# A fused attention and squared-ReLU kernel: its list of 4,011 steps is written anew

## The chip, the cores and the metric

One core of one Trainium2 chip runs the program. The metric is the device time of one execution in microseconds (us). Each engine takes its instructions strictly in the order in which the program lists them: TensorE (PE, matmuls), VectorE (DVE), ScalarE (ACT), GpSimd (POOL) and SyncE (SP, which issues every DMA). An instruction that waits for another engine holds up all that stands behind it on its own engine.

## The reference

Block-causal attention over 8 batches, 8 heads, 576 positions and 64 dimensions, then a two-layer network with a squared ReLU on its 4,608 rows:

```python
scores = scale * np.matmul(q, k.transpose(0, 1, 3, 2))
mask = block_i >= block_j                     # blocks of 64 positions
attn = softmax(np.where(mask, scores, -1e9))
x = np.matmul(attn, v)                        # rows of 8 heads x 64
h = x @ w_in                                  # 512 -> 2048
r = np.maximum(h, 0.0)
out = (r * r) @ w_out                         # 2048 -> 512
```

## The kernel before

Nearly all matmuls are in float16. A float32 operand is split into a high half and a low rest (`high`, then `low` = value - high), and three products replace one. Much of the work of DVE, ACT and POOL is this splitting.

**Attention** goes in passes of one batch and two heads; passes 0 to 11 (the first keys of batches 0 and 1, and their later keys for batch 0) stay in float32, the rest are split. Of pass `i` and part `n`: `A` are the scores on PE (into the PSUM tiles `side`), `B` the row maximum on DVE (`nmx`), `C` the exponential on ACT, `S` a small step on POOL (`sm`), `R` the reciprocal on DVE (`rs`), `H` and `L` the high and low halves of the probabilities (`p_rows`), `T` a DMA transpose, `G` the product with the values on PE (`px`), `X` its scaling into `x`. `fv`, `fa` to `fe`, `vh` and `vl` scale and split the values.

**Norm and split of a tile of x** (batch `b`, half `g`): `sq` and `sa` square and add (tile `sq`), `nq` sums on PE, `hb` makes a power of two, `xm` multiplies (`x<-x,hb`), then the halves `h` and `l` go to `xt_all`. From the fifth chunk on there are also the sums `s1` to `s4` (tile `s`), which either DVE or POOL makes.

**The first layer** works on twelve chunks of 384 rows. The first four are plain: `ph` (12 matmuls of 384 columns), `pos`, `sqr`, `top` (high half) and `rem` (low half, tile `hidden`). The other eight use seven products `p1` to `p7` in four groups in place of eight, each of 12 matmuls of 192 columns (tiles `group`): `c` copies a product out of PSUM into `r` (ACT or DVE), `a` adds the second product (DVE, `r<-group,rescale,r`), `sq` squares, `top` and `rem` split. `p6` waits for `c11`, `p5` for `a11`, `p7` for `c12`, `p4` for `c22`, `p3` for `a22`. The weights for this are made between chunks 1 and 3 by the steps `t`, on DVE or POOL (tile `_AluOpType.subtract`, then `turned_w` or `w`).

**The second layer** is `po` (three matmuls of 512 columns a step), `ob` (scaling) and `out` (store). The weights themselves are loaded and split at the start by `bits`, `prelu`, `join`, `max`, `cast` and `low`.

**What sets the order** is one string, `ORDER`: 4,011 names of steps, some with the engine behind a colon (`:D` DVE, `:A` ACT, `:P` POOL). `plan_all` registers each step with `add` (engine, length, predecessors `after`, rank, buffers), and `Plan.run` takes the steps out in the order of the string. It reads nothing of a step but the function that issues it:

```python
for word in ORDER.split():
    name, _, way = word.partition(":")
    make = self.tasks.pop(name)[3]
    make(WAYS[way]) if way else make()
```

`add` keeps predecessors and lengths in a record that `run` doesn't read. Every instruction is issued through one line of a helper, L329, so the profile tells steps apart by their tiles. On each engine the instructions are bound to the order of the string; waits between engines follow from the data.

Of the kernel before, what the change touches and what calls it, by code (L numbers as in the profile page):

```python
# [108 lines left out]
r11 Q4:A r12 r13 r14 r15 bits0_10 keys9 bits0_11 max0_10 bits0_13 B8_0 E6 G5 C8_0 hb0_0 S8_0 cast0_0:P E7 clear F6:A B8_1 C8_1 max0_11 S8_1 max0_12
X5_0:A load8 G6 Q5:A bits0_12 max0_13 F7:A max0_14 z0 xm0_0 A8_2 prelu0_7 X6_0:A max0_15 Q6:A G7 w0a1 h0_0 bits0_5 w0b1 X7_0:A Q7:A R8_0 nq1_0 B8_2  # L110
D8_0:A bits0_7 R8_1 w0c1 w0d1 C8_2 S8_2 keys10 l0_0 A9_0 D8_1:A w0e1 hb1_0 low0_0 E8_0_0 E8_0_2 A9_1 R8_2 F8_0_0:A D8_2:P cast0_1:P xm1_0 join0_5
F8_0_2:A E8_1_0 h1_0 B9_0 z1 E8_0_1 l1_0 F8_1_0:A F8_0_1:A bits0_9 E8_1_1 z2 prelu0_8 C9_0 F8_1_1:A B9_1 join0_7 ia1_0 E8_2_0 F8_2_0:A S9_0 w0e C9_1
S9_1 ph0_0 pos0_0 low0_1 bits0_14 E8_2_1 join0_8 A9_2 cast0_2:P R9_0 sqr0_0 F8_2_1:A A10_0 B9_2 join0_6 z3 z4 bits1_0 D9_0:A B10_0 C9_2 prelu0_9 S9_2
low0_2 R9_1 cast0_3:P join0_9 keys11 ph0_1 pos0_1 D9_1:D prelu0_10 R9_2 G8_1 D9_2:P join0_10 A10_1 low0_3 cast0_4:D prelu0_11 prelu0_12 ph0_2 E9_0_0
sqr0_1 top0_1:A C10_0 low0_4 X8_1:A S10_0 cast0_5:P join0_11 prelu0_13 bits1_3 B10_1 pos0_2 join0_12 join0_13 top0_0:D low0_5 E9_0_1 sqr0_2 F9_0_0:A
ph0_3 R10_0 C10_1 S10_1 cast0_6:P prelu0_14 E9_0_2 A10_2 A11_0 F9_0_2:D prelu0_15 join0_14 pos0_3 prelu1_0 bits1_1 F9_0_1:D D10_0:A bits0_15 bits1_2
load11 B10_2 ph0_4 C10_2 join1_0 low0_6 E9_1_0 F9_1_0:A E9_1_1 top0_2:D rem0_1 pos0_4 F9_1_1:A cast0_7:D join0_15 low0_7 sqr0_3 cast0_8:P load9 ph0_5
E9_2_0 E9_2_1 ph0_6 max1_0:A S10_2 R10_1 D10_1:D pos0_5 bits1_4 prelu1_1 F9_2_1:A B11_0 F9_2_0:A sqr0_4 A11_1 G9_1 low0_8 prelu1_2 R10_2 cast0_9:P
load12 join1_1 prelu1_3 E10_0_0 rem0_2 pos0_6 sqr0_6 z5 prelu1_4 D10_2:P ph0_7 C11_0 X9_1:A B11_1 max1_1:D F10_0_0:A E10_0_1 E10_0_2 bits1_5 join1_2
S11_0 prelu1_5 ph0_8 C11_1 pos0_7 low0_9 cast0_10:P F10_0_1:A F10_0_2:A rem0_0 E10_1_0 S11_1 max1_2:D join1_4 top0_6:D sqr0_7 R11_0 join1_3 D11_0:A  # L120
join1_5 low0_10 cast0_11:P max1_5:D R11_1 F10_1_0:A top0_7:D top0_4:D z6 bits1_6 E10_1_1 F10_1_1:A A11_2 sqr0_5 B11_2 A12_0 low0_11 cast0_12:P load10
top0_3:D E10_2_0 rem0_3 top0_5:A E10_2_1 C11_2 z7 bits1_7 F10_2_1:A prelu1_6 S11_2 ph0_9 z8 prelu1_7 pos0_8 pos0_9 F10_2_0:D G10_1 sqr0_8 E11_0_0
B12_0 prelu1_8 max1_4:A X10_1:A bits1_8 low0_12 F11_0_0:A cast0_13:P A12_1 D11_1:D E11_1_0 load13 R11_2 D11_2:P join1_6 z9 vals12 rem0_6 C12_0 E11_0_2
F11_1_0:A bits1_9 join1_7 prelu1_9 S12_0 F11_0_2:A max1_6:A rem0_4 ph0_10 z10 B12_1 E11_2_0 E11_2_1 max1_7:D F11_2_0:A ia0_0 C12_1 A12_2 low0_13
# [1900 lines left out]
```

## Time and profile before

| | us |
|---|---|
| median of three runs | 976.61 (975.47 to 978.28) |
| the profiled execution | 977.2 |
| its span | 975.4 |
| PE busy | 941.6 (97%) |
| DVE busy | 795.4 (82%) |
| ACT busy | 599.8 (61%) |
| POOL busy | 264.5 (27%) |

A view by stretches gives the busy time of each engine and the clock that was granted to PE as a share of the full one. A timeline row gives start, length, engine, operation, tiles, shape and count; in square brackets stands the idle time just before it and what ended it. A row of groups gives the busy time and the mean of one in ns.

### The profile page before, as it was taken

Reading aid. Unit: us, or ns where it says so; the run is one execution under the profiler, and the core shown is the slowest. Engines: PE = TensorE matmul, PEld = TensorE weight load, DVE = VectorE, ACT = ScalarE, POOL = GpSimd, SP = SyncE. Lnnn points to the kernel's source line nnn. Section 1 sums busy time; section 2 is a strip of 40 time slices with the busy share of each in tenths; the row PEclk is TensorE's granted clock in tenths of the full one; section 3 lists DMA queues with packets and bytes.
Section 4 is the critical chain, followed back from the end, with each engine's and each line's share of the span. In section 5 each row is a group of like instructions: output and inputs, shape, how many; then the busy total and the mean of one; then the engine's idle time right before and its main releaser. Section 6 shows DMA issues by size and latency. Waiting matters only on the chain.

```text
span 975.4 us, 20874 instructions
## 1 busy us (share of the span) xinstructions
PE 941.6 (97%) x8001; PEld 593.2 (61%) x8001; DVE 795.4 (82%) x1769; ACT 599.8 (61%) x1510; POOL 264.5 (27%) x366
## 2 busy tenths in 40 slices
...
GB/s 360 326 123 168 163 134 101 165 174 174 83 128 117 122 100 121 111 74 121 148 96 140 41 163 79 153 118 100 91 161 119 90 99 90 79 13 1 23 2 44
DMA packets 221649, 114.92 MB, mean 118 GB/s; under 512 B 195290, under 2 KB 203756, under 8 KB 221548
## 3 DMA queue, kind: packets, MB, share of 16 engines
...
## 4 chain that ended last, share of the span: by engine, by line
PE 72%; DVE 18%; DMA 4%; issue 3%; ACT 2%; POOL 1%; SPq 1%; DVEq 0%; POOLq 0%; ACTq 0%
PE pair L329 37%; PE group L329 21%; PE side L329 7%; DVE p_rows L329 5%; PE px L329 5%; DVE nmx L329 3%; DVE w L329 2%; PE po L329 2%; DMA first<-in_qk 2%; DVE r L329 2%; DVE hidden L329 1%; DMA hidden<-in_w_in 1%; ACT p L329 1%; DVE xt_all L329 1%; DVE x L329 1%
## 5 line engine op out<-in xcount | busy, mean ns | idle before, releaser
L329 PE MATMUL pair<-w,hidden 128*128 128x512 f16 (+1 forms) x1680 | 382.1, 377 | 1.6 <-DVE ob L329 1.6
L329 PEld LDWEIGHTS <-hidden 128*128 128x128 f16 x1776 | 169.5, 98 | 179.7 <-issue 11.8
L329 PEld LDWEIGHTS <-w 128*128 128x128 f16 x2304 | 201.4, 98 | 74.3 <-issue 16.3
L329 ACT ACTIVATE p<-side,nmx 128x256 f32<-128x256 f32 (+8 forms) x264 | 139.7, 538 | 111.7 <-DVE nmx L329 80.5
L329 POOL TENSOR_TENSOR hidden<-r,hidden 128x384 f16<-128x384 f32 x101 | 104.0, 1040 | 228.5 <-ACT hidden L329 216.0
L329 DVE SCALAR_TENSOR_TENSOR p_rows<-p,rs,p_rows 128x128 f16<-128x128 f32 (+6 forms) x264 | 147.5, 581 | 9.8 <-ACT p_rows L329 6.7
L329 PE MATMUL group<-xt_all,w 128*128 128x192 f16 x1536 | 142.9, 246 | 1.6 <-DVE r L329 1.4
L329 DVE TENSOR_REDUCE nmx<-side 128x1 f32<-128x192 f32 (+8 forms) x288 | 123.3, 479 | 18.5 <-PE side L329 18.0
L329 PE MATMUL pair<-xt_all,w 128*128 128x384 f16 x768 | 131.1, 326 | 2.0 <-ACT r L329 1.2
L329 POOL TENSOR_SCALAR sm<-sm 128x2 f32<-128x2 f32 (+2 forms) x104 | 34.3, 330 | 351.6 <-ACT p L329 337.2
L329 ACT ACTIVATE r<-r 128x384 f32<-128x384 f32 x208 | 106.8, 522 | 33.0 <-DVE r L329 30.5
L329 PE MATMUL group<-xt_all,turned_w 128*128 128x192 f16 x1152 | 108.9, 246 | 0.3 <-DVE r L329 0.3
L329 PEld LDWEIGHTS <-turned_w 128*128 128x128 f16 x1152 | 96.1, 98 | 12.2 <-issue 3.5
L329 PE MATMUL side<-qk 64*64 64x512 f32 (+2 forms) x480 | 97.2, 500 | 3.4 <-ACT p L329 1.9
L329 PE MATMUL side<-ks,qk 64*64 64x128 f32 (+4 forms) x576 | 92.3, 425 | 0.1
L329 ACT CAST hidden<-r 128x384 f16<-128x384 f32 x156 | 76.5, 508 | 19.3 <-DVE r L329 17.0
L329 DVE SCALAR_TENSOR_TENSOR r<-group,rescale,r 128x384 f32<-128x384 f32 x96 | 58.3, 612 | 33.7 <-PE group L329 26.8
L329 ACT ACTIVATE r<-group,rescale 128x384 f32<-128x384 f32 x72 | 41.4, 577 | 59.5 <-PE group L329 51.7
L329 ACT ACTIVATE p_rows<-p,rs 128x64 f16<-128x64 f32 (+9 forms) x124 | 61.9, 525 | 19.3 <-DVE rs L329 15.1
L329 DVE TENSOR_SCALAR p_rows<-p,rs 128x384 f16<-128x384 f32 (+9 forms) x156 | 68.6, 456 | 1.8 <-DMA p_turned<-p_rows 0.5
L329 PE MATMUL px<-p_turned,v 128*64 128x384 f16 (+5 forms) x1168 | 67.2, 269 | 1.7 <-ACT wt L329 1.4
L329 PEld LDWEIGHTS <-v 128*64 128x64 f16 x1128 | 49.1, 110 | 21.1 <-issue 8.8
...
## 6 DMA issues: line engine op xcount, KB each, us to landing
...
```

What stands on the lines that cost most here:

```text
L329: i = make(*a, **k)
```

## The change

The string is replaced by another with the same 4,011 names. Half of the names stand over 11 places from where they were, and some change engine: `c` 12 from DVE to ACT, `ob` 6 from DVE to ACT, `sq` 19 from ACT to DVE, `t` 12 and `s` 15 from DVE to POOL, `rem` 3 from DVE to POOL, `H` 16 from DVE to ACT. In all DVE has 1,355 steps where it had 1,410, ACT 944 for 919, and POOL 345 for 315. PE's steps are the same in number and kind. Five places of `plan_all` change what is passed to `add` as predecessors or freed buffers.

```diff
-p0 A0 B0 C0 S0 A1 r0 B1 C1 p1 prelu0_0 r1 A2 r2 prelu0_1 bits0_0 max0_0 S1 R0 prelu0_2 D0:D R1 D1:P p2 r3 B2 C2 bits0_1 A3 bits0_2 S2 bits0_3 B3 C3 E0
...
-                over = {x: [f"po{prev}_2_{4 * g + int(x[1]) + 1}"] for x in ("11", "12", "21", "22")}
+                over = {x: [f"po{prev}_{m}_{4 * g + int(x[1]) + e}" for m in ((0, 1), (1, 2))[int(x[0]) - 1] for e in (-1, 1)] for x in ("11", "12", "21", "22")}
...
-                    ends = [(opener, z) for z in ("xt0", "xt1")] if g == NQ - 1 else []
+                    ends = [(opener, z) for z in ("xt0", "xt1")]
...
-                over = [f"po{prev}_2_{f}"] if ck else []
+                over = [f"po{prev}_{m}_{f}" for m in range(3)] if ck else []
...
-            add(f"X{i}_1", {"ACT": 440, "DVE": 490}, 0, [f"G{i}_1"], base + YR[3], lambda q, t=t: values_out(t, 1, q), frees=[(f"G{i}_1", "x")])
+            add(f"X{i}_1", {"ACT": 440, "DVE": 490}, 0, [f"G{i}_1", "l1_0" if t["b"] == 0 else "l0_1"], base + YR[3], lambda q, t=t: values_out(t, 1, q), frees=[(f"G{i}_1", "x")])
...
-                        if hp == 0:
-                            pb = b - 1 if g else (b - 1 if b > NT else 0)
-                            past = ([f"l{pb}_{g}"] if plain(chunk_of(pb, g)) else [f"l23{pb}_{g}", f"l6{pb}_{g}"]) if pb >= 0 else []
-                        else:
-                            past = []
+                        pb = b - 1 if g else (b - 1 if b > NT else 0)
+                        past = ([f"l{pb}_{g}"] if plain(chunk_of(pb, g)) else [f"l23{pb}_{g}", f"l6{pb}_{g}"]) if pb >= 0 else []
```

The program built from the old code with the new string alone has the same instructions on every engine, row for row, as the one with all of the change.

**First place: POOL at some 397 to 408 us, between the second layer of chunk 4 and the first of chunk 3.** Tiles `t_AluOpType` and `w_107` are the weight steps `t`, `sm` the steps `S`, `s_3_0` the sums of a tile of x. Before:

```order
L329 TENSOR_SCALAR sm_0_0_4_4597<-sm_0_0_4_4597 128x4
L329 TENSOR_TENSOR t_AluOpType.subtract_4485<-t_AluOpType.subtract_4485,w_107 128x512
L329 TENSOR_SCALAR sm_0_0_7_4648<-sm_0_0_7_4648 128x3
L329 TENSOR_TENSOR w_107<-t_AluOpType.subtract_4483,w_107 128x2x256
L329 TENSOR_TENSOR w_107<-t_AluOpType.subtract_4485,w_107 128x2x256
L329 TENSOR_TENSOR s_3_0_4762<-x_97 128x192
L329 TENSOR_TENSOR s_3_0_4787<-s_3_0_4762,x_97 128x192
```

Now, on POOL at the same place of the program:

```order
L329 TENSOR_SCALAR sm_0_0_4_4595<-sm_0_0_4_4595 128x4
L329 TENSOR_TENSOR w_107<-t_AluOpType.subtract_4586,w_107 128x2x256
L329 TENSOR_SCALAR sm_0_0_7_4636<-sm_0_0_7_4636 128x3
L329 TENSOR_TENSOR w_107<-t_AluOpType.subtract_4463,w_107 128x2x256
L329 TENSOR_TENSOR s_3_0_4767<-x_97 128x192
L329 TENSOR_TENSOR s_3_0_4770<-s_3_0_4767,x_97 128x192
L329 TENSOR_TENSOR x_97<-x_97,s_3_0_4770 128x2x96
L329 TENSOR_TENSOR x_97<-x_97 128x2x96
```

Behind the step `S24_1` (`sm_0_0_7`) stand one weight step where there were two, and four sums of x where there were two.

**Second place: DVE at the same time, up to the sums `sq_0_0` that PE's step `nq3_0` waits for.** `p_rows` are the halves of the probabilities. Before:

```order
L329 RECIPROCAL rs_0_0_7_4664<-sm_0_0_7_4648 128x3
L329 TENSOR_SCALAR p_rows<-p_4_0_0_7_4647,rs_0_0_7_4664 128x512
L329 TENSOR_SCALAR p_rows<-p_4_0_0_7_4647,rs_0_0_7_4664 128x384
L329 SCALAR_TENSOR_TENSOR p_rows<-p_4_0_0_7_4647,rs_0_0_7_4664,p_rows 128x384
L329 SCALAR_TENSOR_TENSOR p_rows<-p_4_0_0_7_4647,rs_0_0_7_4664,p_rows 128x512
L329 SCALAR_TENSOR_TENSOR p_rows<-p_4_0_0_4_4596,rs_0_0_4_4627,p_rows 128x320
L329 TENSOR_TENSOR sq_0_0_4717<-sq_0_0_4717 128x384
L329 TENSOR_TENSOR sq_0_0_4717<-sq_0_0_4717 128x192
```

Now, on DVE at the same place of the program:

```order
L329 RECIPROCAL rs_0_0_7_4652<-sm_0_0_7_4636 128x3
L329 SCALAR_TENSOR_TENSOR p_rows<-p_4_0_0_4_4594,rs_0_0_4_4631,p_rows 128x64
L329 TENSOR_SCALAR p_rows<-p_4_0_0_7_4635,rs_0_0_7_4652 128x384
L329 SCALAR_TENSOR_TENSOR p_rows<-p_4_0_0_7_4635,rs_0_0_7_4652,p_rows 128x384
L329 SCALAR_TENSOR_TENSOR p_rows<-p_4_0_0_4_4594,rs_0_0_4_4631,p_rows 128x256
L329 TENSOR_SCALAR x_97<-px_3_0_1_4667,xsc_2_0_3893 128x384
L329 TENSOR_TENSOR sq_0_0_4708<-sq_0_0_4708 128x384
L329 TENSOR_TENSOR sq_0_0_4708<-sq_0_0_4708 128x192
```

The high half of 512 columns has gone to ACT and its low half behind the sums; two shorter low halves and an `X` stand there now.

**Third place: DVE at some 431 to 435 us, in the groups of chunk 3.** `x_97<-x_97,hb_1` is `xm3_1`; the step `a113_2` (`r_3_2_5033` before, `r_3_2_5061` now) is what the product `p53_2` waits for. Before:

```order
L329 SCALAR_TENSOR_TENSOR r_3_1_4927<-group_4772,rescale,r_3_1_4927 128x384
L329 SCALAR_TENSOR_TENSOR r_3_1_4927<-r_3_1_4927 128x384
L329 TENSOR_SCALAR m_0_0_5113<-pm_0_0_4756 128x2
L329 TENSOR_TENSOR x_97<-x_97,hb_1_4989 128x1536
L329 SCALAR_TENSOR_TENSOR r_3_2_5033<-group_4774,rescale,r_3_2_5033 128x384
```

Now, on DVE at the same place of the program:

```order
L329 TENSOR_SCALAR r_3_2_5166<-group_4777,rescale 128x384
L329 SCALAR_TENSOR_TENSOR r_3_2_5061<-group_4778,rescale,r_3_2_5061 128x384
L329 RECIPROCAL rs_1_0_7_5193<-sm_1_0_7_5159 128x3
L329 TENSOR_REDUCE nmx_1_0_8_5196<-side_75 128x1 x2
L329 TENSOR_SCALAR nmx_1_0_8_5196<-nmx_1_0_8_5196 128x2
L329 SCALAR_TENSOR_TENSOR r_3_2_5166<-group_4778,rescale,r_3_2_5166 128x384
L329 SCALAR_TENSOR_TENSOR v_4_0_0_5001<-vraw_90,s_0_0_4955,v_4_0_0_5001 128x640
L329 TENSOR_TENSOR x_97<-x_97,hb_1_5143 128x1536
```

The long multiplication stood just ahead of `a113_2` and stands six rows behind it now.

## Rows read from the trace of the kernel before

**Rows 1.** Page, part 1: busy us (share of the span) and instructions.
```profile
PE 941.6 (97%) x8001; PEld 593.2 (61%) x8001; DVE 795.4 (82%) x1769; ACT 599.8 (61%) x1510; POOL 264.5 (27%) x366
```
**Rows 2.** Stretches: us, busy PE, PEld, DVE, ACT, POOL; PE's clock; DMA.
```profile
0.00:50.00 50.00, 38.25 (x330) 25.43 (x330) 40.66 (x118) 36.76 (x116) 27.01 (x49) 0.93 0.86 335
50.00:117.00 67.00, 60.01 (x439) 32.99 (x440) 66.23 (x125) 60.68 (x148) 50.97 (x59) 1.00 0.49 156
117.00:400.00 283.00, 276.67 (x1994) 143.07 (x1995) 248.33 (x553) 172.72 (x442) 71.22 (x99) 1.00 0.60 131
400.00:410.00 10.00, 7.75 (x59) 3.72 (x56) 9.37 (x19) 5.17 (x11) 4.13 (x5) 0.83 0.00 1
...
450.00:850.00 400.00, 398.56 (x3738) 265.56 (x3733) 339.50 (x774) 248.64 (x637) 81.85 (x122) 1.00 0.56 112
```
**Rows 3.** Timeline at 400 to 410 us: POOL, DVE and PE around step nq3_0.
```profile
400.40 2.46 POOL L329 TENSOR_TENSOR w<-_AluOpType.subtract,w 128x512 f16<-128x512 f32 x2
400.57 2.51 DVE L329 TENSOR_SCALAR p_rows<-p,rs 128x512 f16<-128x512 f32 x2
...
401.84 1.47 PE L329 MATMUL pair<-w,hidden 128*128 128x512 f16 x6
...
405.56 0.24 PE L329 MATMUL nq<-sq,ones_bf 128*128 128x192 bf16 x1 [2.25 <-DVE sq L329]
405.65 4.31 PE L329 MATMUL pair<-w,hidden 128*128 128x512 f16 x12
```
**Rows 4.** Timeline at 300 to 306 us, around step nq2_1.
```profile
301.77 1.28 POOL L329 TENSOR_TENSOR turned_w<-_AluOpType.subtract,turned_w 128x512 f16<-128x512 f32 x1 [1.48 <-ACT turned_w L329]
301.96 1.15 DVE L329 TENSOR_SCALAR p_rows<-p,rs 128x64 f16<-128x64 f32 x1
...
305.09 0.48 PE L329 MATMUL nq<-sq,ones_bf 128*128 128x384 bf16 x2 [1.42 <-DVE sq L329]
```
**Rows 5.** Timeline at 430 to 437 us: DVE and PE around product p53_2.
```profile
432.60 1.75 DVE L329 TENSOR_TENSOR x<-x,hb 128x1536 f32<-128x1536 f32 x1
...
434.27 0.61 DVE L329 SCALAR_TENSOR_TENSOR r<-group,rescale,r 128x384 f32<-128x384 f32 x1
...
434.93 1.15 PE L329 MATMUL group<-xt_all,w 128*128 128x192 f16 x12 [1.37 <-DVE r L329]
```
**Rows 6.** Timeline at 262 to 276 us: PE, two starts of scores.
```profile
264.92 0.49 PE L329 MATMUL side<-qk 64*64 64x320 f32 x2 [0.80 <-ACT p L329]
...
273.11 0.76 PE L329 MATMUL side<-qk 64*64 64x320 f32 x4 [1.01 <-ACT r L329]
...
273.96 0.14 PEld L329 LDWEIGHTS side<-ks,qk 64*64 64x64 f32 x2 [0.65 <-DMA ks<-in_ks]
```
**Rows 7.** Groups of instructions on DVE and POOL: busy us, mean ns, idle before.
```profile
L329 DVE TENSOR_TENSOR hidden<-r,hidden 128x384 f16<-128x384 f32 x91 | 55.3, 616 | 7.3 <-ACT hidden L329 6.9
L329 DVE TENSOR_SCALAR r<-group,rescale 128x384 f32<-128x384 f32 x56 | 34.2, 610 | 10.2 <-PE group L329 10.1
L329 DVE SCALAR_TENSOR_TENSOR r<-r 128x384 f32<-128x384 f32 x46 | 27.4, 599 | 1.2 <-ACT r L329 0.7
L329 DVE TENSOR_TENSOR _AluOpType.subtract<-_AluOpType.subtract,w 128x512 f32<-128x512 f32 x15 | 10.2, 683 | 0.1
L329 POOL TENSOR_TENSOR _AluOpType.subtract<-_AluOpType.subtract,w 128x512 f32<-128x512 f32 x13 | 17.0, 1306 | 40.6 <-DVE _AluOpType.subtract L329 30.0 <-DVE turned_w L329 10.3
```
**Rows 8.** Timeline at 858.5 to 863 and 882 to 885.5 us: PE and DVE in groups.
```profile
860.12 1.15 PE L329 MATMUL group<-xt_all,w 128*128 128x192 f16 x12
...
861.11 2.06 PE L329 MATMUL group<-xt_all,turned_w 128*128 128x192 f16 x23
...
882.51 1.46 PE L329 MATMUL pair<-w,hidden 128*128 128x512 f16 x6
...
882.71 0.62 DVE L329 SCALAR_TENSOR_TENSOR r<-group,rescale,r 128x384 f32<-128x384 f32 x1 [0.89 <-PE group L329]
```

More of the change, by code (lines that the diff above doesn't have):

```diff
@@ L109 @@
[L109 to L124, printed above, removed]
@@ new lines @@
+F7:A max0_13 X4_0:A E6 G7 F6:A max0_10 X7_0:A Q4:A S8_0 Q7:A max0_11 max0_14 S8_1 R8_1 R8_0 G6 X6_0:A max0_15 A8_2 Q5:A Q6:A bits0_9 B8_2 w0a1 nq1_0
+clear load11 D8_0:A bits0_11 xm0_0 w0b1 A9_0 z2 w0c1 hb1_0 w0d1 C8_2 cast0_1:P D8_1:A w0e1 S8_2 h0_0 R8_2 E8_0_0 E8_0_1 xm1_0 F8_0_0:A E8_0_2 F8_0_1:A
+h1_0 A9_1 E8_1_0 F8_0_2:A B9_0 bits0_15 l0_0 l1_0 B9_1 D8_2:P E8_2_0 C9_0 low0_1 ph0_0 F8_1_0:A join0_6 prelu0_8 bits1_1 bits0_7 S9_0 keys10 bits1_2
+R9_0 w0e F8_2_0:A E8_2_1 bits0_14 A9_2 join0_8 C9_1 B9_2 F8_2_1:A prelu0_9 A10_0 cast0_2:P D9_0:A load9 S9_1 pos0_0 C9_2 E8_1_1 F8_1_1:A keys11 R9_1
@@ new lines @@
+low0_2 load8 sqr0_0 join0_7 B10_0 ph0_1 D9_1:A prelu0_10 pos0_1 join0_9 cast0_3:P prelu0_11 A10_1 ia1_0 low0_3 bits1_0 S9_2 ph0_2 B10_1 join0_10 R9_2
+cast0_4:P low0_4 join0_11 G8_1 C10_0 prelu0_12 cast0_5:D pos0_2 A10_2 join0_12 X8_1:A low0_5 z3 B10_2 D9_2:P prelu0_13 E9_0_0 E9_0_1 sqr0_1 prelu0_14
+top0_1:D join0_13 F9_0_0:A F9_0_1:D C10_1 ph0_3 prelu0_15 S10_0 E9_1_0 R10_0 F9_1_0:A cast0_6:P A11_0 low0_6 E9_1_1 join0_14 prelu1_0 z4 rem0_1 pos0_3
+bits1_4 join0_15 join1_0 top0_0:D E9_0_2 F9_1_1:A cast0_7:P ph0_4 load12 prelu1_1 D10_0:A pos0_4 F9_0_2:A low0_7 C10_2 S10_1 B11_0 prelu1_2 E9_2_0
@@ new lines @@
+L23_0_4 po4_1_8 po4_1_9 R23_1 H23_1_2:D H23_1_1:D L23_1_1 L23_0_2 t1_14:P t1_15:P X21_0:A po4_1_10 po4_1_11 po4_1_12 po4_1_13 po4_1_14 L23_0_1 G22
+C23_2 po4_1_15 L23_1_2 S23_2 R23_2 H23_2_1:D H23_1_0:A T23_0_1 L23_1_0 A24_0 ob4_1:D H23_2_0:A X22_1:A po4_2_0 po4_2_1 po4_2_2 T23_0_0 po4_2_3 po4_2_4
+t0_13:P B24_0 C24_0 t0_14:P A24_1 po4_2_5 po4_2_6 t0_15:D T23_1_0 X22_0:D po4_2_7 po4_2_8 L23_2_0 t0_16 L23_2_1 B24_1 S24_0 R24_0 H24_0_2:D T23_1_1
+C24_1 po4_2_9 t0_17:P H24_0_0:D L24_0_0 t1_16 H24_0_1:D L24_0_1 H24_0_3:D H24_0_4:D S24_1 R24_1 G23 X23_0:A A25_0 L24_0_4 sq3_0_0 H24_1_1:D L24_1_1
@@ new lines @@
+po6_1_11 po6_1_12 fv34 R34_2 H35_0_1:D X33_0:A H35_0_3:D A35_1 po6_1_13 po6_1_14 po6_1_15 L35_0_1 fv35 fa34 H34_2_0:D L35_0_3 L34_2_0 H34_2_1:A
+L34_2_1 p78_1 fb34 p28_1 H35_0_0:A B35_1 fc34 fd34 top118_0 L35_0_0 c228_1:A ob6_1:A H35_0_4:A p58_0 a228_0 L35_0_4 p48_1 po6_2_0 po6_2_1 po6_2_2
+po6_2_3 po6_2_4 H35_0_2:A L35_0_2 fe34 rem118_0:P a118_1 T34_1_0 T34_1_1 vh34:D C35_1 c218_1:A sq228_0:D vl34 S35_1 R35_1 A35_2 p38_0 sq218_1:D
+sq118_1:A H35_1_0:D B35_2 H35_1_1:A H35_1_2:A L35_1_2 L35_1_1 p58_1 a228_1 top228_0 top118_1 G34 C35_2 a128_0 T35_0_1 S35_2 R35_2 L35_1_0 A36_0
```

389 lines of the change are left out of this document (195 added, 194 removed).

## The prediction

> **What bounds the kernel now.** I read the page's busy shares first. PE is busy for 941.6 of the 975.4 us [rows 1], so what a new order can give back is at most PE's idle time, 33.8 us, and what PE loses at a lower clock. The second view says where that idle time lies. The reader is to subtract PE's busy time from each stretch [rows 2]: 11.8 us up to 50 us, 7.0 from 50 to 117 (where the second chunk starts), 6.3 from 117 to 400, 2.3 between 400 and 410, and only 1.4 in the 400 us from 450 on; the rest lies between 410 and 450 and at the end. So the new list can't be worth anything in the long second part, where PE has nothing to wait for, and its gain or loss is made in the first 450 us.
>
> Then the same rows are read across [rows 2]. From 50 to 117 us DVE is busy for 66.2 of 67.0 us: there it is DVE that sets the pace, and PE's 7 us are a consequence. From 117 to 400 DVE is busy for 88% of the time and ACT for 61%. A queue that full has no room for a step that comes late, and the timeline shows four such places.
>
> At 405.56 PE has waited 2.25 us for the sums of squares [rows 3]. The cause stands 5 us earlier: two conversions on DVE took 2.51 us beside two GpSimd steps that took 2.46 us. And the wait costs twice. The granted clock of that stretch is 0.83 on average [rows 2], and the twelve matmuls behind the wait took 4.31 us, where six of the same kind just before it took 1.47 [rows 3]. They ran on the lower of the two levels (1.2 GHz in place of 2.4) after PE had stood still: 4.3 - 2.9 = 1.4 us lost.
>
> At 305.09 PE waited 1.42 us for the sums of the next tile, after a 64-column conversion on DVE had taken 1.15 us beside a GpSimd step of 1.28 [rows 4]. At 434.93 it waited 1.37 us for a sum that DVE could start only at 434.27, behind a multiplication of 1.75 us [rows 5]. At 264.92 it waited 0.80 us to write scores into a PSUM tile from which ACT had not finished reading, and at 273.11 1.01 us; there the next row on weights names the landing of the keys [rows 6], so I hold a late load to be the cause.
>
> **The change part by part.** The edits of `plan_all` cost nothing and give nothing: `run` reads the names, the engines and the functions, not the predecessors. All that can act is the string.
>
> *Steps that change engine.* DVE loses 12 `c` at 0.610 us and 12 `t` at 0.683 [rows 7], 7.3 + 8.2 = 15.5 us, and gains 19 `sq` at 0.599, 11.4 us. The other moves come to 55 - 5 = 50 steps fewer; at DVE's mean of 795.4 / 1769 = 0.45 us that is 22.5 us. So DVE has some 27 us less to do, 3.4% of its busy time. POOL gets 30 steps more, near 1.0 to 1.3 us each [rows 7], some 30 us. Neither is a term of its own: from 450 us on, nobody waits for DVE, and before that the relief shows only where a wait is taken away.
>
> *What a GpSimd step costs DVE.* The two places above show a DVE step held for nearly the whole of the GpSimd step beside it [rows 3, 4]. The Trainium skill has a rule for this ("SBUF — State Buffer", section "Who interferes with whom"): the two engines share a port pair that is locked for a whole instruction, and the one that issues second is blocked fully. On average the trace shows far less: the subtractions that make the low halves, 91 of them on DVE, have a mean of 0.616 us [rows 7], which leaves no room for a hold of a microsecond in more than a few. The bounds for 30 steps more are 0 and 30 us of DVE time. I take a quarter, 8 us, since most steps meet no GpSimd step in POOL's 27% [rows 1]; DVE keeps a relief of some 19 us.
>
> *The wait at 405 us.* POOL has one weight step behind `S24_1` now where there were two, and the conversion of 512 columns, the one that was held, has gone to ACT. Ahead of the sums DVE has five shorter steps. PE's own order there is unchanged, and of the two conversions that took 2.51 us one is left. I take 2.0 of the 2.25 us and all of the 1.4 us at the lower clock: -3.4. The bounds are 0, if another GpSimd step comes to lie beside them, and -3.7.
>
> *The wait at 305 us.* The sums stand ahead of the small conversions now, and the second-largest weight step isn't beside them. -1.2, bounds 0 and -1.4.
>
> *The wait at 434 us.* The multiplication stands six rows behind the sum that PE needs. What is late next is the sum itself, and PE has one more product step of the second layer ahead of it. -1.4, bounds -0.8 and -1.4.
>
> *The scores at 264 and 273 us.* In the new list three `ph` blocks lie between the last exponential and the scores that write its tile, where there was none. The load of the keys of pass 21 is listed further ahead of its scores than before (16.9 us of PE's work in place of 6.1, by PE's steps between the two). -1.8, bounds 0, if the load is held up in SP's queue again by the step ahead of it, and -1.8.
>
> *The first 117 us.* The list gives DVE less to do ahead of the second chunk: `D9_1` goes to ACT, `D0` to POOL, and two low halves (2 x 0.616 = 1.2 us [rows 7]) stand behind it; `cast` changes places two for two. With the two conversions, which I estimate at 0.6 us a step from the same rows, that is 1.2 + 1.2 + 0.6 = 3.0 us on an engine that is 99% busy [rows 2]. But the 11.8 us up to 50 us hang on loads and on chains over three engines, of which I see no clear gain or loss. Bounds 0 and -3.0; I take -2.0.
>
> *Tighter products.* This is the part that speaks against the change. In the eight group chunks a product must wait for a step of DVE or ACT on an earlier product. I counted in the lists how often only one other product lies between the two. Before that is so once, with ACT; now it is so 21 times, 16 of them with DVE. One product lasts 861.11 - 860.12 = 0.99 us from start to start [rows 8]. The answer takes: from the start of PE's next work to DVE's start 882.71 - 882.51 = 0.20, the step itself 0.62 [rows 8], and from DVE's end to the start of a PE that waits 434.93 - 434.88 = 0.05 [rows 5], in all 0.87. So 0.12 us are to spare, if DVE is free at that moment. If it has just begun another step, up to 0.6 us is lost (bounds for 16: 0 and +9.6; ACT has the same spare and is emptier). DVE is busy for 85% of the time there [rows 2], but the new list puts short or early steps ahead of many of these; I take 0.15 us each: +2.4.
>
> *New waits elsewhere.* All of the list is new, and it will have places of its own where a step comes late. From 117 to 410 us the old one had 8.6 us of them [rows 2]. Bounds 0 and +8.6; I take +2.0, since DVE has 3% less to do while PE has the same. The sums `s` on POOL in place of DVE are longer, which delays a tile by about a microsecond; second-layer steps and the first two products of a group, 2 x 0.99 us, cover it, and without that cover it would be part of this term.
>
> The sum, against the profiled execution's 977.2 us (the span and 1.8 us around it): 977.2 - 3.4 - 1.2 - 1.4 - 1.8 - 2.0 + 2.4 + 2.0 = 971.8. The median of the three runs, 976.6, is 0.6 us below that execution, so I predict 971.2 us, 0.55% less.
>
> **The rivals.**
>
> *Slower, by the tight products.* Place: the 21 products of chunks 3 and 5 to 11. Each wait also pushes all that DVE and ACT are to do for the next product. It decides against the change from (7.8 + 2.9) / 21 = 0.51 us a place on, where 7.8 is the gain without this term and 2.9 the 0.3%: that is one DVE step in front each time. At 0.8 us, a step that a GpSimd step holds as well: 976.6 - 7.8 + 16.8 = 985.6 us. For it: DVE is 85% busy, POOL gets 30 us more. Against it: the answer fits into 0.99 us, and the one place that was as tight before (at 861.11, behind ACT) had no wait [rows 8].
>
> *No change.* The waits at 264 to 434 us go, and others of the same size take their places, because chains over three engines shift as a whole; the first 117 us stay, because ACT there (60.7 of 67.0 us busy) is nearly as full as DVE. Then only the doubly paid wait at 405 remains, -3.4, and the tight products cost +2.4: 975.6 us.
>
> *No change, by the port.* If each GpSimd step holds one DVE step for its length, the 30 added steps take 30 us from DVE, and the 27 us of relief are gone. The gains of the first 117 us and at 305 and 273 us fall away with it: 971.2 + 2.0 + 1.2 + 1.0 = 975.4 us. This is what the rule of the Trainium skill's "SBUF — State Buffer" ("Who interferes with whom") would make of it; the single rows agree with it, the means don't.
>
> *A larger gain.* All of the 8.6 us from 117 to 410 go, with the 1.4 us at the lower clock and 1.4 at 434, 3.0 us at the start, and the tight products cost nothing: 976.6 - 14.4 = 962.2 us.
>
> **How the numbers follow.** The forecast has 0.53, the larger gain 0.11, no change 0.13, the port 0.09, slower 0.14. About 0.3%, 2.9 us, is what a measurement of this kernel can tell from no change, so faster means below 973.7. Of the forecast some 0.52 of its 0.53 lies there, with the larger gain 0.63; no change and the port are within 0.3% with most of their weight, 0.21; 0.16 is left for slower. The range reaches from the larger gain, 962, to 980: above it lies most of the slower rival, below it half of the larger gain, together less than 0.2.
>
> **What would show it.** PE's idle time from 117 to 450 us should fall from some 10 us to below 5, and the clock of the stretch at 400 to 410 us should be 1.00. DVE's busy time should fall by some 19 us and POOL's rise by some 30. If the tight products cost what I take, PE's waits for `r` in group chunks come to 2 to 3 us; a sum over 8 us is the slower rival. If DVE's steps beside POOL grow so much that its busy time stays near 795, the port decides. PE's busy time far from 942 us would make all of this wrong, since no matmul changes.

## The result, and the profile after

The new kernel takes 966.73 us (median; 966.22 to 967.33), the old one beside it 976.98 (975.47 to 978.28): a ratio of 0.9896, 95% interval 0.9879 to 0.9913. That is 10.2 us, 1.0%, where 5.4 were forecast. The sign is clear, the size nearly twice the forecast.

Part 1 of the page after, in the columns of [rows 1]:

```profile
PE 935.4 (97%) x8001; PEld 591.3 (61%) x8001; DVE 771.2 (80%) x1713; ACT 605.8 (63%) x1522; POOL 289.6 (30%) x396
```

DVE has 24.2 us less to do, POOL 25.1 more, ACT 6.0 more. The span is 965.5 us, 9.9 shorter than in the profiled execution of before, and only 3.7 us of this is idle time of PE. The other 6.2 us are PE's busy time, with the same 8,001 matmuls: the old kernel had two stretches at the lower clock, which by [rows 2] account for 5.2 us of it (0.07 of 50 us and 0.17 of 10). The stretches of the new kernel, to be held against [rows 2] (us, then busy PE, PEld, DVE, ACT, POOL, then PE's clock and the DMA's share):

```profile
0.00:50.00 50.00, 37.66 (x354) 25.22 (x354) 41.92 (x122) 39.91 (x123) 33.10 (x56) 1.00 0.86 334
50.00:117.00 67.00, 61.27 (x442) 34.26 (x441) 65.05 (x127) 61.03 (x150) 46.69 (x53) 1.00 0.48 157
117.00:400.00 283.00, 276.66 (x2019) 143.51 (x2019) 239.05 (x531) 182.25 (x455) 85.84 (x111) 1.00 0.61 132
400.00:410.00 10.00, 9.78 (x112) 8.40 (x111) 9.86 (x22) 6.30 (x18) 7.26 (x8) 1.00 0.22 41
410.00:450.00 40.00, 39.98 (x423) 31.15 (x421) 36.48 (x78) 32.51 (x82) 13.62 (x19) 1.00 0.52 104
450.00:850.00 400.00, 397.81 (x3722) 266.28 (x3720) 324.67 (x746) 245.93 (x621) 83.32 (x130) 1.00 0.51 109
```

The clock is 1.00 in all of them, where it was 0.93 up to 50 us and 0.83 between 400 and 410. That belongs to this execution: the four of the new kernel have a mean granted clock of 1.000, 0.996, 1.000 and 0.995, and take 967.3, 967.1, 966.3 and 966.2 us, so the two with a lower clock aren't the slower ones. And from 117 to 400 us PE is idle for 6.3 us, as before. The old waits there are gone and others have come. A stretch of wall time shows this badly, since the new kernel is elsewhere in its work at the same moment. So I also followed PE's steps by name through both traces and compared when each kernel has the same amount of PE's work behind it, each step counted at its usual length:

| where (time in the old kernel, us) | gain, us | forecast |
|---|---|---|
| up to 57 | -2.8 | -2.0 |
| 57 to 130 | -1.8 | (in the -2.0) |
| scores of passes 19 to 21 and `nq2_1`, 240 to 310 | -4.1 | -3.0 |
| new waits, 310 to 390 | +3.5 | +2.0 |
| `nq3_0`, 405 | -3.4 | -3.4 |
| `p53_2`, 434 | -1.9 | -1.4 |
| from 450 on, mostly a new wait at `G31` | +0.8 | (in the +2.0) |
| the 21 tight products | 0.0 | +2.4 |

(The rest, -0.1, is spread.) The place at 405 us came out as forecast. In the new kernel the sums `nq3_0` start at 397.94, without a wait, right behind the six matmuls ahead of them, and the twelve behind them run at the full clock (2.75 us, where they took 4.31 [rows 3]):

```profile
396.55 1.47 PE L329 MATMUL pair<-w,hidden 128*128 128x512 f16 x6
397.94 0.24 PE L329 MATMUL nq<-sq,ones_bf 128*128 128x192 bf16 x1
398.02 2.75 PE L329 MATMUL pair<-w,hidden 128*128 128x512 f16 x12
```

The new waits are three, on PE's timeline: for the scales `vd` at `fc22`, for the output step `ob4_1` that empties the PSUM tile of `po`, and for a transpose at `G31`. The first two come back in every profile that keeps this part of the new list. The third doesn't: three other kernels with the same steps there wait for 0 to 0.08 us, so it is of this execution.

```profile
312.95 0.16 PE L329 MATMUL pm<-vd,ones_bf 128*128 128x2 bf16 x1 [1.71 <-DVE vd L329]
...
385.75 3.40 PE L329 MATMUL pair<-w,hidden 128*128 128x512 f16 x15 [2.25 <-DVE ob L329]
...
613.25 1.75 PE L329 MATMUL px<-p_turned,v 128*64 128x384 f16 x28 [0.95 <-DMA p_turned<-p_rows]
```

### The profile page after: what moved, and what is told of

Same layout as the page of the kernel before. It is cut to its first block, busy times and chain, and to the rows that moved or that the text cites. A ratio compares the mean times of both kernels' runs of the same rounds, so it can differ in the third digit from the quotient of the medians.

```text
span 965.5 us, 20885 instructions
## 1 busy us (share of the span) xinstructions
PE 935.4 (97%) x8001; PEld 591.3 (61%) x8001; DVE 771.2 (80%) x1713; ACT 605.8 (63%) x1522; POOL 289.6 (30%) x396
## 4 chain that ended last, share of the span: by engine, by line
PE 75%; DVE 15%; ACT 4%; DMA 3%; POOL 2%; issue 2%; SPq 0%; ACTq 0%; DVEq 0%; POOLq 0%
PE pair L329 37%; PE group L329 23%; PE side L329 7%; PE px L329 5%; DVE nmx L329 3%; DVE p_rows L329 3%; DVE w L329 2%; PE po L329 2%; DMA p_turned<-p_rows 1%; ACT p L329 1%; DVE hidden L329 1%; ACT r L329 1%; DVE xt_all L329 1%; DVE stw L329 1%; POOL w L329 1%
## 5 line engine op out<-in xcount | busy, mean ns | idle before, releaser
L329 PEld LDWEIGHTS <-hidden 128*128 128x128 f16 x1776 | 168.9, 98 | 184.7 <-issue 15.3
L329 POOL TENSOR_TENSOR hidden<-r,hidden 128x384 f16<-128x384 f32 x104 | 101.7, 987 | 194.7 <-ACT hidden L329 178.9
L329 DVE SCALAR_TENSOR_TENSOR p_rows<-p,rs,p_rows 128x128 f16<-128x128 f32 (+7 forms) x264 | 147.5, 581 | 9.4 <-ACT p_rows L329 4.4
L329 POOL TENSOR_SCALAR sm<-sm 128x2 f32<-128x2 f32 (+2 forms) x104 | 31.5, 302 | 348.5 <-ACT p L329 315.1
L329 ACT CAST hidden<-r 128x384 f16<-128x384 f32 x160 | 79.2, 508 | 43.9 <-DVE r L329 35.2
L329 ACT ACTIVATE p_rows<-p,rs 128x64 f16<-128x64 f32 (+11 forms) x142 | 73.8, 544 | 29.7 <-DVE rs L329 24.3
L329 ACT ACTIVATE r<-r 128x384 f32<-128x384 f32 x168 | 85.8, 521 | 10.3 <-DVE r L329 8.6
L329 ACT ACTIVATE r<-group,rescale 128x384 f32<-128x384 f32 x84 | 48.2, 577 | 68.1 <-PE group L329 62.9
L329 PEld LDWEIGHTS <-v 128*64 128x64 f16 x1128 | 49.2, 110 | 24.2 <-issue 12.2
L329 DVE TENSOR_TENSOR hidden<-r,hidden 128x384 f16<-128x384 f32 x88 | 52.7, 613 | 9.0 <-ACT hidden L329 8.9
```

Source lines behind the costliest of these rows:

```text
L329: i = make(*a, **k)
```

## The experiments

Each kernel was timed beside the old one. Where I speak of a gain "in the trace", it is the comparison at equal work of PE, as in the table.

**Order and engines apart.** 504 of the 4,012 steps (the list has one more than the 4,011 given above) stand on another engine in the new list, most of them in exchange (64 `H` go from DVE to ACT, 48 the other way). One kernel takes the old order with the new engines, one the new order with the old engines:

```diff
-p0 A0 B0 C0 S0 A1 r0 B1 C1 p1 prelu0_0 r1 A2 r2 prelu0_1 bits0_0 max0_0 S1 R0 prelu0_2 D0:D
+p0 A0 B0 C0 S0 A1 r0 B1 C1 p1 prelu0_0 r1 A2 r2 prelu0_1 bits0_0 max0_0 S1 R0 prelu0_2 D0:P
```

> The old list, row for row, with each step on the engine that the new list gives it. Theory A (the relief of DVE by 27 us is itself worth something in the 99% busy start and at the late sums): 972 to 975 us. Theory B (an engine is only right together with the place; a step that goes to ACT or GpSimd at a place that was tuned for DVE comes late for somebody): slower than the old kernel, 978 to 985 us.

Measured: 1020.0 us, a ratio of 1.0456 (1.0426 to 1.0487).

> The new list, row for row, with each step on the engine of the old list. Theory A (the order makes the gain, the engines add little): 967 to 970 us. Theory B (order and engines only work together): 974 to 985 us.

Measured: 1024.7 us, 1.0504 (1.0477 to 1.0531). Both A theories fall, and both are worse than any B had it. Of the first kernel, the stretch from 450 to 850 us:

```profile
450.00:850.00 400.00, 381.51 (x3610) 259.62 (x3610) 317.21 (x728) 244.72 (x622) 85.24 (x128) 1.00 0.51 106
```

PE stands idle for 18.5 us there, where the old kernel has 1.4 and the new one 2.2, though DVE is no fuller (317 of 400 us, in the new kernel 325). Such a list is an order for one assignment. With 504 steps on engines that are sensible on average, but each meant for another place, the loss is 43 us, some 0.09 us a step, and it is spread: 6 us by 117 us, 10 more by 400, and 22 between 450 and 850. Which of the steps cost it was not separated, and some of it is the clock, whose mean is 0.990 and 0.985 in these two profiles and 0.995 in the old kernel's. So the sums of durations that I made for DVE and POOL say nothing on the result by themselves.

**Cut at 117 us.** At `w1e` the two lists have issued the same steps but for 17. One kernel takes the new list up to there and the old one behind, the other the reverse:

```diff
 w1d fd12 H12_2_0:A rem0_9 ph1_2 S13_0 top0_11:A pos1_1 w1e
-L12_2_0 rem0_10 cast1_0:A H12_2_1:A rem0_11 T12_0_0 fe12 low1_0 ph1_3
+T12_1_1 H12_2_1:A L12_2_0 T12_0_0 L12_2_1 rem0_10 rem0_11 fe12 sqr0_14
...
```

> The first 581 steps of the new list (to `w1e`, some 117 us), then all that is left in the old list's order, with the old engines. The first stretch of the new list gave 4.7 us in the trace. Theory A (the gain of the start is a gain of its own, since the second chunk can start earlier and all behind it shifts with it): 977 - 4.7 = 972.3 us. Theory B (the start only buys time that a load or a chain over three engines takes back behind it): 975.5 to 977 us.

Measured: 974.3 us, 0.9980 (0.9964 to 0.9995).

> The first 592 steps of the old list (to `w1e`), then what is left in the new list's order, with the new engines. Theory A: the new list without its start, 966.7 + 4.7 = 971.4 us, and the lower clock at 36 to 45 us is back. Theory B: within 1 us of the new kernel, 966 to 968 us.

Measured: 972.1 us, 0.9959 (0.9945 to 0.9972). The second agrees with A: without its start the new list is 5.4 us slower. In the traces 4.3 us of this are there at 130 us; 1.7 more come at 390 us, where PE runs at the lower clock behind the wait for `ob4_1` (last section). The first gives only 2.3 us, between A and B, in executions from 972.5 to 978.1. The profiled one is the last of these, and its mean clock (0.991) is the lowest of the ten; the five with 0.998 take 972.5 to 974.4. Its trace shows the full gain by 118 us, a loss of 1.3 us right at the cut, and a loss of 2.9 us at 266 to 280 us. There the scores of pass 21 now wait for 2.26 us, 1.25 more than before, and the matmuls behind them run at the lower clock:

```profile
264.80 0.38 SPq L329 DMA_DIRECT2D qk<-in_qk  x1
265.24 1.34 SPq L329 DMA_DIRECT2D ks<-in_ks  x1
...
270.90 0.76 PE L329 MATMUL side<-qk 64*64 64x320 f32 x4 [2.26 <-ACT r L329]
```

What is gained earlier is of no use where a load is issued only just ahead of the scores that need it. In the new list the same load (the second pair of rows) is issued 16 us ahead of its scores, which start at 270.10 without a wait:

```profile
252.44 0.59 SPq L329 DMA_DIRECT2D qk<-in_qk  x1
253.44 0.33 SPq L329 DMA_DIRECT2D ks<-in_ks  x1
253.86 0.38 SPq L329 DMA_DIRECT2D qk<-in_qk  x1
254.30 0.42 SPq L329 DMA_DIRECT2D ks<-in_ks  x1
```

**The load alone.** In the old list the load is issued behind four loads of values, 4.9 us ahead of its scores, which start at 273.11 [rows 6]:

```profile
268.26 0.39 SPq L329 DMA_DIRECT2D qk<-in_qk  x1
268.71 0.40 SPq L329 DMA_DIRECT2D ks<-in_ks  x1
```

One step is moved:

```diff
-L19_0_1 B19_2 R19_1 rem2_1:P ... A20_0 L19_1_1 vals20 load21 H19_1_0:A
+L19_0_1 B19_2 load21 R19_1 rem2_1:P ... A20_0 L19_1_1 vals20 H19_1_0:A
```

> The old list with one step moved: `load21`, the load of the queries and keys of pass 21, stands behind `B19_2`, ahead of the four loads of values that it queued behind on SP. Theory A (the waits at 270 to 274 us, 1.2 and 0.8 us, are for this load): both go, the time is 975.0 us, 2.0 less. Theory B (the scores wait for ACT to read the PSUM tile, as the row's releaser says, and for the load only by the way): 976 to 977 us, the 1.2 us stay.

Measured: 972.9 us, 0.9963 (0.9950 to 0.9975). PE's timeline has the scores at 270.83 with a wait of 0.17 us:

```profile
256.79 0.36 SPq L329 DMA_DIRECT2D qk<-in_qk  x1
257.20 0.42 SPq L329 DMA_DIRECT2D ks<-in_ks  x1
...
270.83 0.49 PE L329 MATMUL side<-qk 64*64 64x320 f32 x2 [0.17 <-ACT p L329]
```

A holds for the wait: the releaser in [rows 6] (`<-ACT r`) was not what PE waited for; the load was. Its time, 975.0, is missed by 2.1 us. In the trace the move is worth 1.6 us. The two profiled executions are 4.3 us apart; of the rest, 1.3 us are the clock at 405 us (last section) and 1.4 us the start, and the move touches neither. But all six executions (972.4 to 973.6) are faster than all fifteen of the old kernel beside them (974.1 to 977.9), so chance alone is a weak reason for the 2 us, and where they come from is not shown. The start, for one, isn't the same in every execution. Four other kernels with the old start stand 1.1 to 2.0 us earlier at 57 us than the profiled execution of before, so a part of the 2.8 us in the table's first line belongs to that one execution.

**The sums at 405 us.** In the old list three weight steps are moved, so that GpSimd would be idle beside the two conversions (`t3_16` between the other two is ACT's):

```diff
-L24_0_3 H24_0_4:A t2_17:P t3_16 t3_17:P R24_1 T23_1_1 G23 ... L24_0_4 sq3_1_1 out4_1 po4_2_11 nq3_0
+L24_0_3 H24_0_4:A R24_1 T23_1_1 G23 ... L24_0_4 sq3_1_1 t2_17:P t3_16 t3_17:P out4_1 po4_2_11 nq3_0
```

> The old list with three steps moved: the weight steps `t2_17`, `t3_16` and `t3_17` stand behind the sums `sq3_1_1`, so that GpSimd is idle while DVE makes the two conversions ahead of `nq3_0`. Theory A (the conversions took 2.5 us because of the GpSimd steps beside them, and the clock fell because PE waited for that): the wait of 2.25 us falls below 1 us, the clock stays at 1.00, 973.5 to 975 us. Theory B (the weights, late now, hold product `p13_0` instead): the wait moves to 410 to 415 us, 976 to 979 us.

Measured: 976.0 us, 0.9997 (0.9987 to 1.0007). Neither came true. GpSimd, DVE and PE around `nq3_0`:

```profile
399.16 1.16 POOL L329 TENSOR_TENSOR w<-_AluOpType.subtract,w 128x512 f16<-128x512 f32 x1
399.33 1.60 DVE L329 TENSOR_SCALAR p_rows<-p,rs 128x512 f16<-128x512 f32 x2
...
402.62 1.51 DVE L329 TENSOR_TENSOR sq<-sq 128x384 bf16<-128x384 bf16 x2
402.87 1.15 POOL L329 TENSOR_TENSOR w<-_AluOpType.subtract,w 128x512 f16<-128x512 f32 x1 [2.55 <-ACT w L329]
...
404.28 0.24 PE L329 MATMUL nq<-sq,ones_bf 128*128 128x192 bf16 x1 [2.23 <-DVE sq L329]
```

The edit did only half of what it was to do. `t2_17` starts at 399.16 all the same, because no other step of GpSimd stands ahead of it: a place further back in the list holds a step up only behind steps of its own engine or behind data. `t3_17` came later, since it waits for ACT's `t3_16`. So the first conversion still takes 1.27 us and the second 0.41, where it took 1.31: both together fell from 2.51 to 1.60 us, and GpSimd did hold the second. But `t3_17` now lies beside the two additions of the sums, and they take 1.51 us, where two such took 0.64 before. The wait is 2.23 us, as it was (2.25). The step that was taken away from one link of DVE's chain was given to another.

The new list doesn't keep GpSimd away from this chain either. One of its conversions takes 1.34 us beside a weight step:

```profile
394.28 1.16 POOL L329 TENSOR_TENSOR w<-_AluOpType.subtract,w 128x512 f16<-128x512 f32 x1 [0.31 <-ACT w L329]
394.32 1.34 DVE L329 TENSOR_SCALAR p_rows<-p,rs 128x384 f16<-128x384 f32 x1
```

What ends the wait is that the chain, from `R24_1` to the end of the sums, is shorter (3.8 us for 5.1) and starts earlier (3.9 us ahead of the moment at which PE is ready for `nq3_0`, for 3.0). The two differences, 1.3 and 1.0 us, are the 2.25 us.

**DVE's work in the start, taken away and put back.** The old list with part of what the new one takes from DVE ahead of `w1d` taken away (3.4 us, steps added up), and the new list with such work put back (4.4 us). The first edit is shown; the second puts `D0`, `D9_1` and `H12_0_1` back on DVE and three low halves ahead of `w1d`:

```diff
-... D9_0:A B10_0 C9_2 prelu0_9 S9_2 low0_2 R9_1 cast0_3:P join0_9 keys11 ph0_1 pos0_1 D9_1:D
+... D9_0:A B10_0 C9_2 prelu0_9 S9_2 low0_2 R9_1 cast0_3:P join0_9 keys11 ph0_1 pos0_1 D9_1:A
...
-sqr0_11 L12_2_0 ph1_1 T12_1_0 T12_0_0 sqr0_10 L12_2_1 top0_10:A w1b w1c top0_11:D ph1_2 rem0_10 rem0_11 w1d
+sqr0_11 ph1_1 T12_1_0 sqr0_10 top0_10:A w1b w1c top0_11:D ph1_2 w1d ... w1e L12_2_0 L12_2_1 T12_0_0 T12_1_1 T12_0_1 rem0_10 rem0_11
```

> The old list with DVE's work ahead of the second chunk (`w1d`) lightened as the new list lightens it, and nothing else: `D9_1` goes to ACT (1.32 us on DVE in the trace), and `L12_2_0`, `L12_2_1`, `rem0_10`, `rem0_11` stand behind `w1e` (2.1 us together). Theory A (DVE sets the pace of the first 117 us, so what is taken from it there is time): 977 - 3.4 = 973.6 us. Theory B (ACT and the chains over three engines are as late as DVE): 976 to 978 us; the low halves that come late hold the products of pass 12 behind 117 us.

Measured: 977.2 us, 1.0008 (0.9999 to 1.0018): B.

> The new list with DVE's work ahead of `w1d` made heavier by what the new list had taken away: `D0`, `D9_1` and `H12_0_1` are DVE's again, and `H12_2_0`, `H12_2_1`, `L12_2_0`, `L12_2_1`, `rem0_10` stand ahead of `w1d` as in the old list. By the trace of the old kernel that is 0.56 + 1.32 + 0.90 + 0.54 + 0.48 + 0.54 = 4.3 us of DVE. Theory A (the gain of the start is DVE's lighter work): 966.7 + 4.3 = 971.0 us, at least 969. Theory B (the kernel with the lightened old start says that this work is not what the start waits for; it is the order of the chains over DVE, ACT and PE): 966 to 968 us.

Measured: 971.7 us, 0.9945 (0.9929 to 0.9962), 5.0 us above the new kernel: A. In the new list DVE's work is the pace: with 4.4 us more of it, `w1d` starts 3.3 us later (121.18 for 117.86). Of these 1.2 us stand already at 96 us, and 2.1 come at two waits for DVE's small steps `st` and `dg_w`. The rest of the 5.0 us is mostly the lower clock in this execution: the 36 matmuls behind `w1d` take 7.55 us for 6.02, and at `ob4_1` (last section) 1.5 more are lost. First the heavy start, then the new kernel:

```profile
118.97 0.27 PE L329 MATMUL pm_w<-ident,st 128*1 128x128 f32 x1 [1.55 <-DVE st L329]
...
121.18 0.16 PE L329 MATMUL pm_w<-dg_w,ones_bf 1*128 1x1 bf16 x1 [1.93 <-DVE dg_w L329]
121.27 7.55 PE L329 MATMUL pair<-xt_all,w 128*128 128x384 f16 x36
```

```profile
116.52 0.27 PE L329 MATMUL pm_w<-ident,st 128*1 128x128 f32 x1 [0.29 <-DVE st L329]
...
117.86 0.16 PE L329 MATMUL pm_w<-dg_w,ones_bf 1*128 1x1 bf16 x1 [1.06 <-DVE dg_w L329]
117.95 6.02 PE L329 MATMUL pair<-xt_all,w 128*128 128x384 f16 x36
```

In the old list the same relief gives nothing: `w1d` is 1.6 us earlier than in the trace of before, but that kernel was 1.6 us earlier already at 49 us, ahead of the first step that was changed, and a wait of 0.81 us has come behind it:

```profile
122.99 0.17 PE L329 MATMUL pm_w<-dg_w,ones_bf 1*128 1x1 bf16 x1
123.09 2.12 PE L329 MATMUL pair<-xt_all,w 128*128 128x384 f16 x12
126.03 2.11 PE L329 MATMUL pair<-xt_all,w 128*128 128x384 f16 x12 [0.81 <-ACT r L329]
```

So DVE's lighter load is needed for the gain of the start, and the part of it that was tried doesn't bring it alone: `D0` and `H12_0_1` (1.5 us) stayed on DVE here. Which part of the new order makes the relief count was not separated.

**No product between.** In the new list 16 of the 21 tight products are put right behind the product whose answer they need, and so is one more (`p210_3`) that had scores in between:

```diff
-p79_0 sq119_0:A p59_0 h67_0:A l67_0 c229_0:D p49_0
+p79_0 sq119_0:A c229_0:D p49_0 p59_0 h67_0:A l67_0
...
```

> The new list with the one product that stands between a product and the one that needs its answer taken out, at 18 of the 21 tight places: the later product stands right behind the earlier one. Theory A (the answer takes the 0.87 us that the prediction adds up from three rows, since DVE and ACT are free at all of these places): 18 x 0.87 = 15.7 us more, 982.4 us, each wait of PE 0.8 to 0.9 us. Theory B (DVE has mostly just begun another step, as the prediction's +2.4 us supposes, 0.15 us a place on average and up to 0.6): waits between 0.9 and 1.5 us, 985 to 994 us.

Measured: 986.4 us, 1.0103 (1.0083 to 1.0123). Groups of PE (busy us, mean ns, idle before), first of this kernel, then of the new one:

```profile
L329 PE MATMUL group<-xt_all,w 128*128 128x192 f16 x1536 | 142.3, 246 | 8.2 <-DVE r L329 8.0 <-DVE xt_all L329 0.2
L329 PE MATMUL group<-xt_all,turned_w 128*128 128x192 f16 x1152 | 109.5, 246 | 7.9 <-DVE r L329 4.7 <-ACT r L329 3.1
```

```profile
L329 PE MATMUL group<-xt_all,w 128*128 128x192 f16 x1536 | 142.5, 246 | 0.2 <-DVE xt_all L329 0.2
L329 PE MATMUL group<-xt_all,turned_w 128*128 128x192 f16 x1152 | 108.6, 246 | 0.3 <-ACT r L329 0.3
```

In these rows, where the ends of matmuls are modelled, the waits are 15.6 us longer (8.2 + 7.9 - 0.5). From start to start nineteen products wait now. Of the seventeen that were put right behind, sixteen wait for 0.83 to 0.98 us and one for 1.23; two others, which still have a product in between, wait for two steps in a row (1.40 and 1.55). That is 18.5 us together, and the lower clock behind the wait for `ob4_1`, which none of the moves touches, adds 1.6 in this execution. The two profiled executions are 18.8 us apart and the medians 19.7, since the start and the wait at `G31` happen to be shorter here. So A holds for the price of an answer, 0.87 us, at sixteen places of seventeen. Its sum doesn't: 986.4 lies in B's range, 4 us above A's 982.4.

**Cut at 302 us.** At `C21_1` the lists differ by two steps:

```diff
 po2_0_9 po2_0_10 po2_0_11 po2_0_12 po2_0_13 t1_11 t1_12:P po2_0_14 C21_1
-vals22 fv22 fv23 ia2_1 po2_0_15 ob2_0:A ib4 t2_0:D t2_1:D t2_2:D
+po2_1_12 po2_1_13 xm2_1 h2_1 po2_0_15 ob2_0:A vals22 A20_2 B20_2 fv22
...
```

> The new list up to `C21_1` (some 302 us), the rest in the old list's order on the old engines; the two lists have issued the same steps there but for two. Theory A (each place gives its own gain, and they add up): the new kernel's gain up to there, 8.8 us in the trace, 977 - 8.8 = 968.2 us, with the old waits at 405 and 434 us back. Theory B (what the start gains is held up behind it, as in the kernel cut at 117 us): 971 to 974 us.

Measured: 966.7 us, 0.9904 (0.9885 to 0.9923). A holds, with 1.5 us to spare; in its profile the clock didn't fall at 405 us (last section). Within the spread of these executions (966.1 to 968.4) all of the change's gain is made in the first 302 us: behind them the old list is as good as the new one, which gains at 405 and 434 us about what it loses at 310, 384 and 612.

**The new waits mended.** Three of the new list's own:

```diff
-T20_1_1 B21_2 load23 h2_1 fa22 fb22 R21_1 ... po2_2_10 fc22 fd22 L21_1_0 l2_1 ... po2_2_11
+T20_1_1 fa22 fb22 B21_2 load23 h2_1 R21_1 ... po2_2_10 L21_1_0 l2_1 ... po2_2_11 fc22 fd22
...
-A24_0 ob4_1:D H23_2_0:A
+A24_0 ob4_1:A H23_2_0:A
...
-po7_2_4 G31 R32_0 ... po7_2_5 po7_2_6 po7_2_7
+po7_2_4 po7_2_5 po7_2_6 G31 R32_0 ... po7_2_7
```

> The new list with its three largest new waits mended: `fa22 fb22` ahead of `B21_2` on DVE and `fc22 fd22` one product later on PE (1.9 us at 310), the output step `ob4_1` on ACT in place of DVE (2.3 us at 384), two output products ahead of `G31` (1.1 us at 612). Theory A (nothing waits behind these, PE is the bound): 966.7 - 4.8 = 961.9 us. Theory B (the steps they pass come late in turn): 964 to 968 us.

Measured: 968.7 us, 0.9925 (0.9899 to 0.9950), 2.0 us above the new kernel and above B's range. The wait at `fc22` is gone and a longer one has come behind it:

```profile
317.03 0.15 DVE L329 TENSOR_SCALAR m<-pm 128x2 int32<-128x2 int32 x1
317.24 3.57 PE L329 MATMUL px<-p_turned,v 128*64 128x384 f16 x30 [3.49 <-DVE m L329]
```

By putting off `fd22` with `fc22` I moved a step of DVE of 0.15 us behind `L21_1_0`, `l2_1`, `R21_2` and `H21_2_1`, and `G20` on PE waited for it. Behind that wait PE ran at the lower clock: 30 such matmuls took 3.57 us, where 28 take 1.75 in the row at 613.25 above. I had costed where `fc22` stands on PE, and not where its partner comes to stand on DVE. The output step on ACT took its 2.25 us away, but the scores behind it then waited 1.40 us for ACT. At `G31` there was no wait, as in other kernels that left the place alone.

**Four pieces.** From the cuts:

```diff
 (new) ... t1_12:P po2_0_14 C21_1
+(old) po2_1_12 po2_1_13 xm2_1 ... H24_0_2:A po4_2_8 C24_1
+(new) t2_17:D T23_1_1 po4_2_9 ... top125_2 out3_1 fv29
+(old) sq225_2:A top225_2 po5_0_3 ...
```

> Four pieces, taken where the two lists have issued nearly the same steps: the new list to `C21_1` (302 us), the old one to `C24_1` (some 390 us), the new one to `fv29` (some 510 us), the old one to the end. By the two traces each piece is the better one of its stretch: the gain of 9.5 us up to 302 us, none to 390, 3.4 us at 405 and 1.9 us at 434, none behind. Theory A (the pieces add up): 977 - 14.8 = 962.2 us. Theory B (a cut costs what its two sides have promised each other, as the cut at 117 us cost 1.3 us; or the lower clock comes at another wait): 964 to 967 us.

Measured: 964.4 us (963.1 to 964.7), 0.9879 (0.9862 to 0.9895). It lies in B's range, at its lower end: in the trace the first three pieces bring 15.3 us by 470 us, half a microsecond more than expected, and the cut at `fv29` costs 1.1 us. Against the new kernel the runs don't overlap (966.2 to 967.3), but the two ratios to the old kernel do in their intervals, so this is the fastest kernel here by some 2 us, and not by a measured ratio. Its stretch from 400 to 410 us:

```profile
400.00:410.00 10.00, 10.00 (x120) 8.28 (x118) 8.92 (x22) 8.59 (x21) 3.40 (x7) 1.00 0.22 41
```

## Why the prediction was right, and which terms were off

The direction held, and so did the argument for it: what can be gained lies ahead of 450 us, and each gain is the end of one wait. But the sum of -5.4 us is made of terms that err both ways, and that it came out within a factor of two is partly luck.

**The start, -2.0 where -4.6 were measured** (-3.5 when the profiled execution of before is replaced by the mean of the four kernels with the same start, -4.3 against the kernel with the old start and the new rest), outside the bounds of 0 to -3.0. The step "3.0 us on an engine that is 99% busy" counted three moves. By the traces DVE has been busy for 6.4 us less when `w1d` starts (108.2 for 114.6 us). Its steps added up one by one, whose records overlap at their ends, come to 7.5 us less: 4.1 from steps that moved behind or went elsewhere (`D9_1` alone takes 1.32), 3.5 from steps that are shorter. I should have summed DVE's steps ahead of one matmul in both lists. The heavy start shows that this work is time in the new list (3.3 us for 4.4), the light start that 3.4 us of it are worth nothing in the old one; so the step "99% busy, hence time" holds only for an order in which PE waits for DVE there.

**The tight products, +2.4 where nothing was lost.** The count was right and so was the answer, as the kernel without a product between shows. The step that failed is "DVE is busy for 85% of the time there". It is an average, and the list isn't average at these places. DVE stands idle ahead of 15 of the 16, for 0.3 to 2.0 us:

```profile
851.01 1.15 PE L329 MATMUL group<-xt_all,turned_w 128*128 128x192 f16 x12
851.21 0.62 DVE L329 SCALAR_TENSOR_TENSOR r<-group,rescale,r 128x384 f32<-128x384 f32 x1 [0.37 <-PE group L329]
852.00 2.14 PE L329 MATMUL group<-xt_all,w 128*128 128x192 f16 x24
852.20 0.62 DVE L329 TENSOR_SCALAR r<-group,rescale 128x384 f32<-128x384 f32 x1 [0.37 <-PE group L329]
```

DVE has been waiting for PE; it starts 0.20 us after PE has gone on to the product between (852.20 for 852.00), takes 0.62, and the product that needs it starts on time at 852.99. From the end of the step to the start of its product 0.07 to 0.21 us pass at all 21, 0.15 on average. With the 0.05 us of the sum taken off, 0.10 are to spare; the sum had 0.12. The rows of DVE ahead of each place stand in the order and could have been read. The rival that went with this term falls too: waits for `r` in group chunks are 0.3 us, where 2 to 3 were forecast.

**The scores, -1.8 where -3.2 were measured.** The late load was the right cause, and it was two waits, the second (0.65 us for the keys, [rows 6]) uncounted; a wait of 0.5 us at pass 19 went as well. **`nq2_1`**, -1.2, measured -0.9: 0.51 us of the wait are left. **`p53_2`**, -1.4, measured -1.9: with it went a smaller wait of the next product.

**The wait at 405 us, -3.4, hit.** The conversion that went to ACT was the right reading, since the chain is shorter by it. That one GpSimd step less beside the conversions would do is refuted by the kernel with late weights, and the new list itself still has a conversion that is held. The 1.4 us of the clock in this term are luck: they depend on the execution (last section).

**New waits, +2.0 where +4.3 were measured**, within the bounds. The test "idle time from 117 to 450 us below 5" failed by this term: it is 6.6 us.

**The port.** The rival in which 30 more GpSimd steps take 30 us from DVE falls: DVE's busy time fell by 24 us, more than the 19 that I left it. Its low halves have a mean of 613 ns now, 616 before [rows 7], beside 25 us more of GpSimd. Single rows agree with the rule of the Trainium skill ("SBUF — State Buffer", "Who interferes with whom"), the two additions at 402.62 above among them; what was wrong is the rival's reading of it as a price, one held DVE step for each GpSimd step. The means suggest that most of the added steps met no DVE step that they could hold; the overlaps were not counted.

**PE's busy time.** I wrote that a value far from 942 us would make all of this wrong. It is 935.4, and what was wrong is that sentence: PE's busy time holds the time lost to the clock (5.2 of the 6.2 us; the other 1.0 us isn't accounted for). I had read 0.83 at 405 us [rows 2] and passed over the 0.93 ahead of 50 us in the same rows.
